# Earlier filter loads, halved last evacuations, a moved inverse piece and a residual added in PSUM, in a two-layer spectral and dense kernel

## The chip, the cores and the metric

One core of one Trainium2 chip. The metric is the device time of one execution in microseconds (us). The kernel before takes 1016.25 us, the median of three runs (1016.15 to 1018.78). "Span" is the same execution as the profiler sees it, some 2 us shorter.

## The reference

Two layers, each a global spectral filter followed by a feed-forward block, all with residuals. 2048 tokens of 1024 features, 3584 hidden features, bf16.

```python
def _A_ref(x, w_r, w_i):                       # the spectral layer
    X = jnp.fft.rfft2(x.astype(jnp.float32), axes=(-2, -1))
    X = X * (w_r + 1j * w_i)
    return jnp.fft.irfft2(X, s=(S, D), axes=(-2, -1)).astype(jnp.bfloat16)

def _B_ref(x, w1, b1, w2):                     # the dense layer
    h = jnp.einsum("bsd,df->bsf", x, w1) + b1
    sp = jnp.log1p(jnp.exp(-jnp.abs(h))) + jnp.where(h > 0, h, jnp.zeros_like(h))
    return jnp.einsum("bsf,fd->bsd", h * jnp.tanh(sp), w2)

x = x + _A_ref(_layernorm(x), A_w_r, A_w_i)
x = x + _B_ref(_layernorm(x), B_w1, B_b1, B_w2)
x = x + _A_ref(_layernorm(x), A_w_r, A_w_i)    # the same weights again
x = x + _B_ref(_layernorm(x), B_w1, B_b1, B_w2)
```

## The kernel before

The spectral layer is a transform in four stages on TensorE, in eight groups. The inverse's first stages (i1, i2) of the last group, number 7, end the steady part. Their output U goes to DRAM and comes back turned (UT), since the last inverse stage (i4) contracts over what U has in its partitions. Group 6 makes the same trip just before:

```python
def u_turn(g, half):
    u = U[g % 3]
    if g == 7:
        h = slice(8 * half, 8 * half + 8)
        if half == 0:
            u_back(6)                          # SyncE: group 6's 512 KB back from DRAM
        self.dma(act, self.u_d[g][:, h, :], u.ap[:, h, :], ...)   # ScalarE: store half of group 7
        if half:
            u_last()                           # six reads of what was stored
    elif half:
        self.dma(sp, self.u_d[g], u.ap, ...)
        if g:
            u_back(g - 1)
```

Each group's PSUM is copied out by one instruction of two banks, on ScalarE or VectorE, and the filter weights of group g + 2 are loaded when group g is done with its buffer (two buffers in turn):

```python
        # i1
            self.op(act, lambda e: e.activation(v.ap[:, :, i, :], src, ACT.Copy), reads=banks, parts=[v.res])
        # i2
            if (g, half) in ((3, 1), (5, 1), (7, 1)):
                self.op(dve, lambda e: e.tensor_copy(dst, ps), reads=banks, parts=[u.res])
            else:
                self.op(act, lambda e: e.activation(dst, ps, ACT.Copy), reads=banks, parts=[u.res])
        # the loop over stages, first layer
                    filter_bins(g)
                    if g < 6:
                        load_w(g + 2)
```

Before i4, TensorE writes the first four token tiles into PSUM as the residual (`residual_first`), and i4 accumulates on them in quarters, as UT's quarters land. The other twelve tiles' columns are done in pieces (`rest`) that fill gaps of the dense layer's start:

```python
        self.spin(8, 0)                        # dummy matmuls, keep TensorE busy
        self.residual_first()
        # ... (cut) ... layer_B starts:
        for u in range(4):
            self.i4(0, 4, 32 * u, 32, 2 * u)
            self.out_first(u, 0, act)
            # ... (cut: statistics)
        for u in range(4):
            self.out_first(u, 2, (act, act, act, dve)[u])
        self.root(0, 2)
        rest(0)
        rest(3)
        for j in range(2):
            xn[j] = self.apply(j)              # normalize
        for j in range(2):
            transposed(0, j, xn[j])            # TensorE transposes, then the first dense matmuls
```

The joint to the second spectral layer: the last token tile's second half is added to the residual by VectorE, its statistics taken, it is normalized, and 16 small copies turn it for the second layer's first stage.

```python
            self.group(fns, reads=ra + r_w2, writes=[self.r_bank[bank]])    # 28 matmuls
            xs = self.XS[:, j, h * 512:(h + 1) * 512]
            self.op(dve, lambda e: e.tensor_tensor(xs, PS[:, bank, :], xs, ALU.add), ...)
            # ... (cut: statistics, then for the last tile)
                b = self.apply(j, out=True)
                self.xr_direct(j, b)           # 16 DMAs on three queues
```

## Time and profile before

In the kernel before (span 1013.1 us):

| stretch, from the trace | us |
|---|---|
| start to the first second-stage matmul ("prologue") | 38.72 |
| from there to the first of the last group's 16 i1 matmuls ("steady", first layer) | 60.72 |
| from there to the first dense matmul ("tail", first layer) | 24.31 |
| first dense layer, to the end of its last product | 395.00 |
| "joint", to the first matmul of the second spectral layer | 7.00 |
| first stage of that layer | 9.91 |
| steady, second layer | 54.70 |
| tail, second layer | 24.49 |
| second dense layer | 395.01 |
| last add and store | 3.21 |

The two dense stretches are 790 us in which TensorE waits for 0.38 us once in each, and otherwise not. The change can only touch the other 223. The view by stretches of 4 us (span of time, its length, busy us and instructions of TensorE, of its weight loads, VectorE, ScalarE and GpSimd, then the granted clock, DMA share, GB/s):

```profile
112.00:116.00 4.00, 2.64 (x86) 2.29 (x85) 0.76 (x2) 0.91 (x2) 0.00 (x0) 0.91 0.32 71
116.00:120.00 4.00, 2.33 (x64) 2.23 (x61) 3.38 (x11) 3.15 (x7) 0.00 (x0) 0.50 0.98 270
120.00:124.00 4.00, 3.06 (x40) 2.87 (x38) 2.58 (x5) 3.54 (x3) 0.00 (x0) 0.73 1.18 293
```

The third number from the right is the clock: half speed from 115.30 to 122.12, while TensorE waits, transposes, and waits again.

### The profile page before, as it was taken

How to read it: one execution, taken by the hardware profiler on the slowest of the kernel's cores; microseconds unless marked ns; L12 is line 12 of the kernel's file. 1: busy time of each engine (PE TensorE's matmuls, PEld its weight loads, DVE VectorE, ACT ScalarE, POOL GpSimd, SP SyncE). 2: the span in 40 equal slices, each digit the busy share in tenths (PEclk: the TensorE clock that was granted, in tenths of full speed). 3: DMA queues.
4: the chain of work that ended last, by engine and by line, in shares of the span. 5: the costliest groups of instructions: out<-in, count | busy, mean ns of one | idle time of the engine just before them, and what ended most of it. 6: DMA issues, size and time to landing. Idle time of an engine off the chain costs nothing.

```text
span 1013.1 us, 13670 instructions
## 1 busy us (share of the span) xinstructions
PE 952.0 (94%) x5749; PEld 506.0 (50%) x5833; DVE 323.9 (32%) x673; ACT 348.7 (34%) x484; POOL 81.6 (8%) x114
## 2 busy tenths in 40 slices
PE   1799799999999999999999978999999999999998
PEld 0576575444444444444456747644444444444443
DVE  7797468002443000033347736830011100000111
ACT  7898474340000343300029848533100023430000
POOL 4651000000000000002421100000000000000000
PEclk9999899999999999999999999999999999999999
DMA  9979813652110220002922875256411212100000
GB/s 284 248 231 321 217 47 115 204 194 61 47 47 30 76 81 21 1 21 90 196 58 83 233 188 156 75 163 201 129 25 45 74 52 83 42 1 11 21 28 25
DMA packets 154205, 107.00 MB, mean 106 GB/s; under 512 B 74448, under 2 KB 133664, under 8 KB 154144
## 3 DMA queue, kind: packets, MB, share of 16 engines
q1 hardware_dynamic: 143056, 78.61, 27.4%
q0 software_dynamic: 8912, 25.84, 8.8%
q10 hardware_dynamic: 2176, 1.66, 0.5%
q8 instruction: 47, 0.77, 0.3%
q14 instruction: 14, 0.11, 0.0%
HBM read 80.85 MB, written 20.71 MB: 100 GB/s over the span
## 4 chain that ended last, share of the span: by engine, by line
PE 87%; DMA 4%; SPq 3%; DVE 2%; ACT 2%; issue 1%; POOL 0%; ACTq 0%; DVEq 0%
PE PS L1067 38%; PE PS L1050 38%; SPq L249 3%; PE PS L771 2%; PE PS L697 2%; PE PS L792 2%; PE PS L961 2%; DMA ARENA<-in_A_w_i_dram 1%; DMA ARENA<-u_scratch 1%; DMA ARENA<-c_bt 1%; DMA u_scratch<-ARENA 1%; PE PS L1016 1%; PE PS L743 1%; ACT ARENA L778 1%; PE PS L810 1%
## 5 line engine op out<-in xcount | busy, mean ns | idle before, releaser
L1050 PE MATMUL PS<-ARENA 128*128 128x512 bf16 (+1 forms) x1950 | 389.1, 358 | 3.8 <-DVE ARENA L1021 1.9
L1067 PE MATMUL PS<-ARENA 128*128 128x512 bf16 x1756 | 385.5, 379 | 1.9
L1054 ACT ACTIVATE ARENA<-PS,B 128x512 bf16<-128x512 f32 (+1 forms) x248 | 159.4, 645 | 412.1 <-PE PS L1050 411.6
L1050 PEld LDWEIGHTS PS<-ARENA 128*128 128x128 bf16 x1984 | 193.0, 98 | 194.7 <-DVE ARENA L1021 2.9
L1067 PEld LDWEIGHTS PS<-ARENA 128*128 128x128 bf16 x1792 | 175.3, 98 | 211.4
L1072 DVE TENSOR_TENSOR XS<-PS,XS 128x512 bf16<-128x512 f32 x64 | 44.3, 692 | 586.9 <-PE PS L1067 586.9
L460 DVE BATCH_NORM_STATS2 BN<-XS 128x6 f32<-128x512 bf16 x100 | 64.6, 674 | 5.4 <-DMA XS<-in_A_x_dram 4.3
L249 POOL DMA_DIRECT2D xn_scratch<-ARENA x12 | 6.5, 541 | 374.2 <-DVE ARENA L512 374.2
L771 PE MATMUL PS<-ARENA 128*128 128x256 bf16 x256 | 32.4, 273 | 4.0 <-DVE ARENA L760 3.2
L778 ACT ACTIVATE ARENA<-PS 128x1024 bf16<-128x1024 f32 x32 | 33.1, 1054 | 6.8 <-PE PS L771 6.8
L432 ACT ACTIVATE RS<-MV,EPS 128x2 f32<-128x2 f32 (+2 forms) x5 | 1.5, 297 | 96.8 <-DVE MV L463 96.2
L697 PE MATMUL PS<-FD,ARENA 128*128 128x256 bf16 (+1 forms) x256 | 31.8, 271 | 2.4 <-ACT ARENA L617 1.2
L749 ACT ACTIVATE ARENA<-PS 128x1024 bf16<-128x1024 f32 x32 | 32.5, 1044 | 4.5 <-PE PS L745 4.5
L771 PEld LDWEIGHTS PS<-ARENA 128*128 128x128 bf16 x256 | 24.2, 98 | 11.8 <-DVE ARENA L760 5.5
L753 DVE TENSOR_TENSOR ARENA<-ARENA 128x1024 bf16<-128x1024 bf16 x32 | 22.0, 688 | 20.4 <-ACT ARENA L749 20.2
L961 PE MATMUL PS<-MT,ARENA 128*128 128x32 bf16 (+1 forms) x512 | 21.4, 199 | 7.1 <-DMA ARENA<-u_scratch 3.8
L697 PEld LDWEIGHTS PS<-FD,ARENA 128*128 128x128 bf16 x256 | 24.4, 98 | 6.5 <-DVE ARENA L619 1.4
L820 ACT ACTIVATE ARENA<-PS 128x1024 bf16<-128x1024 f32 x26 | 26.8, 1066 | 2.4 <-PE PS L792 2.4
L792 PE MATMUL PS<-ARENA,BD 128*128 128x256 bf16 x192 | 24.9, 273 | 2.3 <-ACT ARENA L778 2.3
L512 DVE TENSOR_SCALAR ARENA<-XS,MV,RS 128x1024 bf16<-128x1024 bf16 x48 | 25.0, 545 | 1.0
L961 PEld LDWEIGHTS PS<-MT,ARENA 128*128 128x128 bf16 x512 | 20.0, 102 | 9.8 <-issue 4.5
L732 ACT ACTIVATE ARENA<-PS 128x1024 bf16<-128x1024 f32 x22 | 22.9, 1058 | 3.1 <-PE PS L697 3.1
(79 smaller groups left out, 516.5 us busy)
## 6 DMA issues: line engine op xcount, KB each, us to landing
ARENA<-in_B_w_dram SPq DMA_DIRECT2D x56, 512.0 KB, 3.9
ARENA<-in_B_w_dram SPq DMA_DIRECT2D x56, 256.0 KB, 4.2
u_scratch<-ARENA SPq DMA_DIRECT2D x14, 512.0 KB, 4.4
ARENA<-u_scratch SPq DMA_DIRECT2D x14, 512.0 KB, 6.1
w_scratch<-ARENA POOLq DMA_DIRECT2D x8, 512.0 KB, 5.8
ARENA<-w_scratch POOLq DMA_DIRECT2D x8, 512.0 KB, 5.2
out_dram<-XS SPq DMA_DIRECT2D x16, 256.0 KB, 2.1
ARENA<-xn_scratch POOLq DMA_DIRECT2D x15, 256.0 KB, 10.6
```

What stands on the lines that cost most here:

```text
L249: return eng.dma_start(out_ap, in_ap).then_inc(ds.sem, 16)
L460: self.op(self.dve, lambda e: e.bn_stats(self.BN[:, j, 6 * h:6 * h + 6], self.XS[:, j, 512 * h:512 * h + 512]), reads=[self.r_xs[j]], part ...
L697: fns.append(lambda e: e.matmul(dst, at(r), FD[:, t:t + n], start=start, stop=stop))
L749: self.op(act, lambda e: e.activation(x.ap.rearrange("p a b -> p (a b)"), ps, ACT.Copy, scale=SIG), reads=banks, writes=[x.res])
L771: fns.append(lambda e, c=c, part=part: e.matmul(ps[:, c * 256:(c + 1) * 256], yk.ap[:, part, c * P:(c + 1) * P], t[:, (128, 0)[part]:(384, ...
L778: self.op(act, lambda e: e.activation(v.ap[:, :, i, :], src, ACT.Copy), reads=banks, parts=[v.res])
L792: fns.append(lambda e, dst=dst, part=part, c=c: e.matmul(dst, BD[:, c:c + P], mov(kd, part), start=(part == 0), stop=(part == 1)))
L961: fns.append(lambda e, l=l: e.matmul(self.PS[:, bank + l // k, l % k * w:(l % k + 1) * w], self.UT.ap[:, u0 + l, :], self.MT[:, 8 * lo:8 * ...
L1050: fns.append(lambda e, db=db, bank=bank, fl=fl: e.matmul(PS[:, bank, 0:w], wb.ap[:, db, fl * P:(fl + 1) * P], x.ap[:, db, tok], start=(db ...
L1054: self.op(act, lambda e, bank=bank, ft=ft: e.activation(at.ap[:, ft, tok], PS[:, bank, 0:w], ACT.Mish, bias=self.B1[:, ft:ft + 1]), reads= ...
L1067: fns.append(lambda e, i=i, ft=ft: e.matmul(PS[:, bank, :], at.ap[:, ft, t * P:(t + 1) * P], W2[ft].ap[:, h * 512:(h + 1) * 512], start=(i ...
L1072: self.op(dve, lambda e: e.tensor_tensor(xs, PS[:, bank, :], xs, ALU.add), reads=[self.r_bank[bank]], writes=[self.r_xs[j]])
```

## The change

Four independent pieces, all against waits of a microsecond or less: (a) filter groups 2 and 3 are loaded into free space before the steady part starts, and the spin goes from 8 matmuls to 4; (b) the last group's evacuations of PSUM are split in two halves, one on VectorE and one on ScalarE; (c) one `rest` piece moves behind the first transposes; (d) the last tile's residual is added by one TensorE matmul against the identity, its statistics are read from PSUM, and the normalized tile is written in two halves. The diff, cut to its core (cuts marked):

```diff
 (a)
+    def wr(self, g):
+        return self.WX[g - 2] if g in (2, 3) else self.WR[g % 2]
 ...
+        if li == 0:
+            self.WX = [self.alloc(f"WX{i}", o["UT"] + 4096 * i, [2, 2, 512]) for i in range(2)]
+            for g in (2, 3):
+                load_w(g)
 ...
-                    if g < 6:
+                    if g in (0, 1):
+                        load_w(g + 4)
+                    elif g in (4, 5):
                         load_w(g + 2)
 ...
-        self.spin(8, 0)
+        self.spin(4, 0)
 (b)
+            if g == 7:                         # in i1
+                for b, prog in enumerate((dve, act)):
+                    self.copy(prog, v.ap[:, 4 * b:4 * b + 4, i, :], src[:, 4 * b:4 * b + 4, :], [banks[b]], [], parts=[v.res])
+                return
 ...
+            def last_out(b, prog):             # in i2
+                r = 8 * half + 4 * b
+                self.copy(prog, u.ap[:, r:r + 4, :].rearrange("p a b -> p (a b)"), ps[:, 512 * b:512 * b + 512], [banks[b]], [], parts=[u.res])
 ...
+            if g == 7:
+                last_out(0, dve)
+                last_out(1, act)
+                return
-            if (g, half) in ((3, 1), (5, 1), (7, 1)):
+            if (g, half) in ((3, 1), (5, 1)):
 (c)
         rest(0)
-        rest(3)
         for j in range(2):
             xn[j] = self.apply(j)
         for j in range(2):
             transposed(0, j, xn[j])
         self.warm(ACT.Mish)
+        rest(3)
 (d)
+            summed = not last and (j, h) == (15, 1)
 ...
+            if summed:
+                self.group([lambda e: e.matmul(PS[:, bank, :], self.IDENT[:], self.XS[:, j, 512:1024], start=False, stop=True)],
+                           reads=[self.r_xs[j], self.r_ident], writes=[self.r_bank[bank]])
+                self.finish_last(bank)
+                return
 ...
+    def finish_last(self, bank):
+        self.op(dve, lambda e: e.bn_stats(self.BN[:, j, 6:12], ps), reads=[rb], parts=[r])
+        self.op(dve, lambda e: e.bn_aggr(self.MV[:, j, :], self.BN[:, j, :]), reads=[r], writes=[r])
+        self.root(j, 1)
 ...
+        for h in range(2):
+            src = ps if h else self.XS[:, j, 0:512]
+            self.op(dve, lambda e, h=h, src=src: e.tensor_scalar(..., src, mean, rs, op0=ALU.subtract, op1=ALU.mult), ...)
+            self.xr_direct(j, b, range(4, 16) if h else range(4))
+        self.copy(self.act, self.XS[:, j, 512:1024], ps, [], [rb, self.r_xs[j]])
```

More of the change, by code (lines that the diff above doesn't have):

```diff
@@ L531, in xr_load, with xr_direct @@
                  reads=[self.r_xnd[j]], parts=self.r_xr[1:3])
-    def xr_direct(self, j, b):
-        b.unread = False
-        for i in range(16):
+    def xr_direct(self, j, b, rows):
+        for i in rows:
             half, h = i // 8, i % 8
@@ L541, in xr_direct @@
                      reads=[b.res], parts=[self.r_xr[2 * half]])
+    def finish_last(self, bank):
+        j, dve, ps = 15, self.dve, self.PS[:, bank, :]
+        rb, r = self.r_bank[bank], self.r_mv[15]
+        self.op(dve, lambda e: e.bn_stats(self.BN[:, j, 6:12], ps), reads=[rb], parts=[r])
+        self.op(dve, lambda e: e.bn_aggr(self.MV[:, j, :], self.BN[:, j, :]), reads=[r], writes=[r])
+        self.root(j, 1)
+        b = self.xn_out[0]
+        assert not b.unread
+        mean, rs = self.MV[:, j, 0:1], self.RS[:, 2, j:j + 1]
+        b.res.begin()
+        for h in range(2):
+            src = ps if h else self.XS[:, j, 0:512]
+            self.op(dve, lambda e, h=h, src=src: e.tensor_scalar(b.ap[:, 512 * h:512 * h + 512], src, mean, rs, op0=ALU.subtract, op1=ALU.mult),
+                    reads=[rb if h else self.r_xs[j], r, self.r_rs[j]], parts=[b.res])
+            self.xr_direct(j, b, range(4, 16) if h else range(4))
+        self.copy(self.act, self.XS[:, j, 512:1024], ps, [], [rb, self.r_xs[j]])
     def pair(self):
@@ L661, in load_w @@
         if self.li == 0:
-            self.load_wr(self.WR[g % 2], g)
+            self.load_wr(self.wr(g), g)
             return
@@ L682, in filter_bins @@
             ps, banks, _ = self.pair()
-            self.filter_bins(g, ps, banks, self.WR[g % 2], WT[2 * g % 8:2 * g % 8 + 2], o["WT"] + 2048 * (2 * g % 8),
+            self.filter_bins(g, ps, banks, self.wr(g), WT[2 * g % 8:2 * g % 8 + 2], o["WT"] + 2048 * (2 * g % 8),
                              self.JT, self.r_jt, dve)
@@ L793, in cls @@
                             dst, BD[:, c:c + P], mov(kd, part), start=(part == 0), stop=(part == 1)))
+            def last_out(b, prog):
+                r = 8 * half + 4 * b
+                self.copy(prog, u.ap[:, r:r + 4, :].rearrange("p a b -> p (a b)"), ps[:, 512 * b:512 * b + 512], [banks[b]], [], parts=[u.res])
             if half == 0:
+                u.res.begin()
                 cls(0, ps[:, 0:256], ps[:, 256:512])
+                if g == 7:
+                    self.group(fns, reads=[v.res, self.r_bd], writes=banks[:1])
+                    fns = []
+                    last_out(0, dve)
                 cls(1, ps[:, 512:768], ps[:, 768:1024])
+                if g == 7:
+                    self.group(fns, reads=[v.res, self.r_bd], writes=banks[1:])
+                    last_out(1, act)
+                    return
             else:
@@ L813, in i2 @@
             self.group(fns, reads=[v.res, self.r_bd], writes=banks)
-            if half == 0:
-                u.res.begin()
+            if g == 7:
+                last_out(0, dve)
+                last_out(1, act)
+                return
             dst = u.ap[:, 8 * half:8 * half + 8, :].rearrange("p a b -> p (a b)")
-            if (g, half) in ((3, 1), (5, 1), (7, 1)):
+            if (g, half) in ((3, 1), (5, 1)):
                 self.op(dve, lambda e: e.tensor_copy(dst, ps), reads=banks, parts=[u.res])
@@ L835, in u_turn, with open_ut @@
                     u_back(g - 1)
+        def open_ut():
+            self.UT = self.alloc("UT", o["UT"], [P, P])
+            self.r_ut = self.sub_res(self.UT, "ut", 4, o["UT"], P * P * 2)
+            for r in self.r_ut:
+                r.begin()
         def u_back(g):
+            if self.UT is None:
+                open_ut()
             self.dma(sp, self.UT.ap[g:P:8, :, :], self.u_d[g].rearrange("l r n -> r l n"), f"usp{g % 3}",
@@ L858, in layer_A @@
         U = ring("U", 3, 4 * K, [16, P])
-        self.UT = self.alloc("UT", o["UT"], [P, P])
-        self.r_ut = self.sub_res(self.UT, "ut", 4, o["UT"], P * P * 2)
-        for r in self.r_ut:
-            r.begin()
+        self.UT = None
+        if li == 0:
+            self.WX = [self.alloc(f"WX{i}", o["UT"] + 4096 * i, [2, 2, 512]) for i in range(2)]
+            for g in (2, 3):
+                load_w(g)
         for stage, g, h in self.order_A():
@@ L1068, in mm2 @@
                     PS[:, bank, :], at.ap[:, ft, t * P:(t + 1) * P], W2[ft].ap[:, h * 512:(h + 1) * 512],
-                    start=(i == 0), stop=(i == NF - 1)))
+                    start=(i == 0), stop=(i == NF - 1 and not summed)))
             self.group(fns, reads=ra + r_w2, writes=[self.r_bank[bank]])
+            if summed:
+                self.group([lambda e: e.matmul(PS[:, bank, :], self.IDENT[:], self.XS[:, j, 512:1024], start=False, stop=True)],
+                           reads=[self.r_xs[j], self.r_ident], writes=[self.r_bank[bank]])
+                self.finish_last(bank)
+                return
             xs = self.XS[:, j, h * 512:(h + 1) * 512]
@@ L1084, in mm2 @@
                     self.root(j, 1)
-                b = self.apply(j, out=True)
-                if j == 15:
-                    self.xr_direct(j, b)
-                else:
-                    self.xn_store(j, b)
+                self.xn_store(j, self.apply(j, out=True))
         w2v = self.w2.rearrange("(ft fp) d -> fp ft d", fp=P)
```

## The prediction

> **What bounds the kernel now.** I read the page's engine shares first, then the chain of waits, then the timeline of the stretches where TensorE isn't dense, then the granted clock there by microsecond. The page says that this is a TensorE kernel:
>
> ```profile
> span 1013.1 us, 13670 instructions
> PE 952.0 (94%) x5749; PEld 506.0 (50%) x5833; DVE 323.9 (32%) x673; ACT 348.7 (34%) x484; POOL 81.6 (8%) x114
> PE PS L1067 38%; PE PS L1050 38%; SPq L249 3%; PE PS L771 2%; PE PS L697 2%; PE PS L792 2%; PE PS L961 2%; DMA ARENA<-in_A_w_i_dram 1%; DMA ARENA<-u_scratch 1%; DMA ARENA<-c_bt 1%; DMA u_scratch<-ARENA 1%; PE PS L1016 1%; PE PS L743 1%; ACT ARENA L778 1%; PE PS L810 1%
> ```
>
> The two dense products (L1050, L1067) are 76% of the chain, some 770 us, and the change leaves them alone but for one matmul. All it can win lies in the rest: the two spectral layers (about 0 to 115 us and 519 to 607 us) and their joints. Four places matter. First, the end of the inverse transform, in the chain of waits:
>
> ```profile
> 102.52 1.03 ACT ARENA L778
> 103.59 1.06 PE PS L792 x8
> 104.68 1.03 ACT ARENA L820
> 105.73 2.89 DMA u_scratch<-ARENA
> 110.00 4.54 DMA ARENA<-u_scratch
> 114.67 2.70 PE PS L961 x96
> ```
>
> Nothing overlaps here: each PSUM copy of about 1.03 us is on the path, and the round trip through DRAM follows. The second spectral layer repeats it (593.45 to 606.90). The other half of the last group goes through VectorE, at 105.67:
>
> ```profile
> 105.67 1.23 DVE L818 CAST ARENA<-PS 128x1024 bf16<-128x1024 f32 x1 [4.30 <-PE PS L810]
> ```
>
> Second, the joint from the dense layer to the next spectral layer, again the chain:
>
> ```profile
> 518.86 0.70 DVE XS L1072
> 519.58 0.70 DVE BN L460
> 520.31 0.22 DVE MV L463
> 520.55 0.30 ACT RS L432
> 520.88 0.17 DVE RS L434
> 521.08 0.56 DVE ARENA L512
> 523.16 2.25 DMA ARENA<-ARENA
> 525.75 0.62 PE PS L611 x8
> ```
>
> Third, the wait for filter weights, in the timeline: TensorE waits 1.10, but ScalarE is idle only from 47.84 to 47.94.
>
> ```profile
> 46.71 1.13 ACT L732 ACTIVATE ARENA<-PS 128x1024 bf16<-128x1024 f32 x1
> 47.29 0.62 PE L922 MATMUL PS<-ARENA 128*128 128x256 bf16 x4 [1.10 <-DMA ARENA<-in_A_w_i_dram]
> 47.94 0.87 ACT L937 ACTIVATE ARENA<-PS 128x384 bf16<-128x384 f32 x2
> ```
>
> Fourth, the start of the dense layer, where the clock is the point (columns of the view by stretches: busy of each engine, then the granted clock):
>
> ```profile
> 120.00:121.00 1.00, 1.00 (x16) 1.00 (x14) 0.98 (x2) 0.56 (x1) 0.00 (x0) 0.50 1.12 285
> 611.00:612.00 1.00, 0.71 (x17) 0.72 (x18) 0.97 (x4) 0.92 (x3) 0.00 (x0) 1.00 1.15 340
> ```
>
> The same matmuls (the inverse pieces of 15) ran at half clock in the first layer, at full clock in the second: 30 of them took 2.58 us and 1.45 us.
>
> [...]0.50 from about 115.4 to 122.1 us (two such windows) and from 606.9 to 610.3 (one), each after TensorE had waited for the round trip. [...]the 16 KB copies at the joint take 2.1 to 2.5 us[...]. [...]The trace: 0.63 us for a 128x512 cast from PSUM against 0.55 for twice as many bf16 elements from SBUF.[...]
>
> **The change part by part.**
>
> *Prefetch of filter groups 2 and 3 into free space.* No bytes are saved; two loads issue at about 37.6 us, when the first stage ends, in place of 40.77 and later, so they land near 43.5 and not at 47.16. TensorE's wait of 1.10 us goes. But ScalarE issues its copies back to back from 47.94 to about 68 and would start only 0.10 to 0.2 earlier. I take 0.15 us. The later wait for an inverse table (0.85 us at 78.19) stays: its load, issued at 68.89, is queued behind group 6's load at 67.45, which waits for group 4's buffer before and after.
>
> *Split of the last evacuations, in both spectral layers.* The copy after i1 of the last group: 1.03 becomes about 0.62 (ScalarE's 128x512 takes 0.60, VectorE's 0.63), saving 0.40. For the first of the two i1 copies VectorE is still busy with products until about 101.4, which is before the second one needs it, so no loss. i2's first half: its first bank is ready after four matmuls; ScalarE starts the second bank where it started the pair, and ends in 0.60 and not 1.02: 0.42 more. i2's second half: 0.63 in place of 1.23, minus about 0.15 as ScalarE first issues the first half's store: 0.45. So both stores start about 0.8 earlier, and the three issues and 4.54 us of reading follow rigidly. 0.8 twice is 1.6 us.
>
> *Spin 8 to 4.* It takes 4 x 0.216 = 0.86 us off TensorE ahead of the residual matmuls, which end at 112.24 while the last quarter lands at 114.54. Not on the path: 0.[...]
>
> *Inverse piece moved behind the transposes, both layers.* Second layer, clock up: the old piece ran (0.73 us) while TensorE would have waited for the normalized tile; behind the transposes it fills the wait for VectorE's copy (613.92 to 614.85, 0.93). One gap for another: 0. ScalarE's table load of 1.28 now precedes its copy of 1.36, the same sum before the first Mish. First layer, clock down: TensorE was behind; 15 matmuls at 0.084 = 1.26 us leave the path to the transposes and refill a 0.9 us gap, so about 0.9 to 1.0 is won, limited by ScalarE. The clock state may differ from run to run, so I take half: 0.5.
>
> *Last tile's residual by TensorE.* Adds one 512-wide matmul, 0.22. Removes the add, 0.70 + 0.02. The statistics from PSUM cost the same 0.70 (my estimate from the add's 0.69 and cast's 0.63 with such a source). The scale-and-subtract of 0.56 becomes one of about 0.3 from SBUF, after which four of the sixteen copies are issued, and 0.63 from PSUM. First issue: 521.66 + 0.22 - 0.72 - 0.26 = 520.90. ScalarE's queue issues its first at 520.9, its second at about 521.55 (data ready at about 521.53), its third at about 522.45 against 523.16. That third one carries the chain: 0.7 us won. The copy of the tile to SBUF by ScalarE is queued behind its DMA issues and ends near 525, before ScalarE is wanted at 526.5: 0.
>
> Sum: 0.15 + 1.6 + 0 + 0.5 + 0.7 = 2.95 us. From the median 1016.25: 1013.3 us, a ratio of 0.997.
>
> **The rivals.** (1) *The round trip doesn't follow its start.* The stores at 105.7 share the DMA engines with the previous group's read-back (DMA share 1.2 to 1.3 from 103 to 107). If that sets when the stores land, the 1.6 falls to about 0.6, and the time is near 1014.3. For it: the store took 2.89 in one layer and 3.65 in the other. Against: the stores are large packets on another queue. (2) *The clock gives it back.* Less spinning and an earlier end of the residual matmuls lengthen the idle stretch, [...]and the first dense matmuls (256 wide, 0.109 each) run at half clock: 16 of them cost 1.75 more per layer. Time 1013 to 1017. For it: the clock already fell in both layers, with spinning. Against: it was up again before the dense matmuls both times. (3) *The prefetch is worth its whole wait*, because TensorE and not ScalarE binds from 47 on (it is 95 to 100% busy there), or the loads crowd out the tables. Gain 1.1 or loss 0.5. Time 1012.3 to 1014. The lack of any ScalarE gap speaks against the gain.
>
> **Range and chances.** All terms together, if each goes well (prefetch 1.1, split 2.0, moved piece 1.2, joint 0.9), give 5.2 us, 1011; all going badly with the clock lost gives about 1017. The three runs before spread over 2.6 us. So 1013.3, with 1010.3 to 1015.8 for 8 in 10. Two per cent would be 20 us, and all waits touched are under 15 us together: faster 0.01, within 2% 0.98, slower 0.01.
>
> **What would show it.** Right: the store of the last group starts about 0.8 us sooner after the last products, in both layers; the first matmul of the second spectral layer starts about 0.7 sooner after the last dense matmul; the wait for filter weights is gone while ScalarE's busy stretch begins less than 0.2 sooner; the moved piece lies in the wait before the first dense matmul. Wrong: the read-back lands at the old time (rival 1); the clock column shows 0.50 in the first dense matmuls (rival 2); the stretch from first s2 to last i2 shrinks by over 0.5 in the first spectral layer apart from the split (rival 3); or the statistics from PSUM take much over 0.7.

(The trace of before showed where the granted clock was 0.50, in "windows" of 3.41 us (the falls took 6.83 and 3.41). The split's 1.6 us took for granted that ScalarE and VectorE can each read a bank of PSUM side by side in the time that one alone takes; that was the author's estimate. After shows it nearly so: at 103.67 both start on a 128x512 piece, and take 0.60 and 0.69 us, where single pieces of that size took 0.60 and 0.63 in before.)

## More of the kernel before

A program on one core has no second core to compare with: runs timed in rounds are all of state fast here, single runs of state unknown, and I say which is which.

To find where time moves, I cut each trace at instructions that both kernels have, so that the stretches add up to the span.

## The result, and the profile after

The changed kernel took 1015.36 us (median of 4 runs, 1015.10 to 1016.42) beside 1016.20 for the kernel before (4 runs, 1014.70 to 1018.78). The ratio is 0.9991, with a 95% interval of 0.9969 to 1.0013. Ratios here are the mean time of one kernel's fast runs over that of the other's fast runs of the same rounds, so not quite the ratio of the medians. On another chip, with six and eleven runs, it came to 0.998 (0.9963 to 0.9997), from 1015.97 and 1017.38 us. So the change wins some 1 to 2 us where I said 2.95: within 2%, inside the range, too optimistic. The first interval includes no change at all, the second just excludes it.

The head of the page after:

```profile
span 1013.4 us, 13752 instructions
PE 958.2 (95%) x5826; PEld 506.4 (50%) x5826; DVE 326.5 (32%) x679; ACT 347.7 (34%) x487; POOL 81.5 (8%) x114
```

This profiled run is 0.3 us *longer* than the one of before. One pair of traces can't carry a difference of 0.1%, and the stretches tell why:

| stretch | before | after | difference |
|---|---|---|---|
| prologue (not touched by the change) | 38.72 | 40.07 | +1.35 |
| steady, first layer | 60.72 | 60.52 | -0.20 |
| tail, first layer | 24.31 | 23.54 | -0.77 |
| first dense layer | 395.00 | 395.01 | +0.01 |
| joint | 7.00 | 6.69 | -0.31 |
| first stage and steady, second layer | 64.61 | 64.61 | 0 |
| tail, second layer | 24.49 | 24.73 | +0.24 |
| second dense layer and end | 398.22 | 398.20 | -0.02 |

The prologue hides the gain. It ends with input loads: the first load of token tiles landed at 3.98 us in the one trace and 4.51 in the other, the last of the eight at 13.89 and 15.27. Over fourteen traces of kernels that all share that code, it took from 38.72 to 40.84 us. I leave it out of every comparison below. Without it, the pair shows -1.04 us.

The chain of waits after, at the end of the first inverse transform (start, length, what):

```profile
102.58 1.06 PE PS L793 x8
...
103.67 0.70 DVE ARENA L572
...
104.42 1.06 PE PS L818 x8
...
105.50 0.61 ACT ARENA L568
...
106.18 3.64 DMA u_scratch<-ARENA
...
111.19 4.02 DMA ARENA<-u_scratch
```

Set it beside the same chain in the prediction. The two copies on the path shrank from 1.03 and 1.03 to 0.70 and 0.61, as meant. But the store, 2.89 before, takes 3.64 now. From the first i1 matmul of the last group, the store starts 0.70 us sooner and lands at 9.24 instead of 9.19.

The joint, in the chain of waits:

```profile
514.81 4.33 PE PS L1121 x20
519.14 0.14 issue
519.28 0.39 PE PS L1127
...
521.20 1.15 DVE ARENA L556 x2
522.34 0.02 issue
522.36 0.75 ACTq L249
523.11 0.03 issue
523.14 2.33 DMA ARENA<-ARENA
```

L1127 is the added matmul. The copy that carries the chain starts 4.01 us after the last product's end, 4.41 before. And the wait for filter weights, which was 1.10 at 47.29, is gone from that place; a smaller one appears later, in the timeline (start, busy, line, then in brackets the wait):

```profile
76.04 0.62 PE L975 MATMUL PS<-ARENA 128*128 128x256 bf16 x4 [0.36 <-DMA ARENA<-in_A_w_i_dram]
```

The clock around the start of the first dense layer, by stretches as before:

```profile
112.00:116.00 4.00, 1.60 (x58) 1.56 (x59) 0.75 (x2) 0.60 (x1) 0.00 (x0) 1.00 0.51 114
116.00:120.00 4.00, 2.26 (x79) 2.00 (x75) 2.54 (x8) 2.93 (x6) 0.00 (x0) 0.58 0.62 180
120.00:124.00 4.00, 3.83 (x46) 3.56 (x45) 3.13 (x8) 3.19 (x5) 0.00 (x0) 0.57 1.18 294
```

The moved piece does what it was to do: TensorE is busy 3.83 of the last 4 us, 3.06 before. It still runs at half clock.

### The profile page after: what moved, and what is told of

It reads as the page before. It is cut to its first block, busy times and chain, and to the rows that moved or that the text cites. A ratio compares the mean times of both kernels' runs of the same rounds, so it can differ in the third digit from the quotient of the medians.

```text
span 1013.4 us, 13752 instructions
## 1 busy us (share of the span) xinstructions
PE 958.2 (95%) x5826; PEld 506.4 (50%) x5826; DVE 326.5 (32%) x679; ACT 347.7 (34%) x487; POOL 81.5 (8%) x114
## 4 chain that ended last, share of the span: by engine, by line
PE 87%; DVE 5%; DMA 4%; ACT 2%; POOL 1%; issue 0%; SPq 0%; ACTq 0%; POOLq 0%; DVEq 0%
PE PS L1121 38%; PE PS L1103 38%; PE PS L793 2%; PE PS L719 2%; PE PS L1014 2%; PE PS L818 2%; DMA XS<-in_A_x_dram 1%; DMA ARENA<-c_bt 1%; POOL ARENA L249 1%; PE PS L1069 1%; DMA ARENA<-u_scratch 1%; DVE ARENA L637 1%; DMA u_scratch<-ARENA 1%; DVE ARENA L775 1%; DVE ARENA L610 1%; ACT ARENA L635 1%
## 5 line engine op out<-in xcount | busy, mean ns | idle before, releaser
L771 ACT ACTIVATE ARENA<-PS 128x1024 bf16<-128x1024 f32 x32 | 33.3, 1071 | 4.5 <-PE PS L767 4.5
L804 ACT ACTIVATE ARENA<-PS 128x1024 bf16<-128x1024 f32 x28 | 29.8, 1087 | 3.9 <-PE PS L793 3.9
L568 ACT ACTIVATE ARENA<-PS 128x1440 bf16<-128x1440 f32 (+1 forms) x22 | 25.5, 1160 | 10.8 <-PE PS L793 3.9
L862 ACT ACTIVATE ARENA<-PS 128x1024 bf16<-128x1024 f32 x24 | 25.3, 1090 | 0.0
```

The costliest lines, as they stand in the source:

```text
L771: self.op(act, lambda e: e.activation(x.ap.rearrange("p a b -> p (a b)"), ps, ACT.Copy, scale=SIG), reads=banks, writes=[x.res])
```

## The experiments

Twelve runs followed: nine new kernels and three repeats. All but two compute the right result. One table holds the stretches of all the traces; each experiment then names the column that decides it. "q" is the time from the last group's first i1 matmul to the first of the last 96 of i4's first 128 matmuls, which work on the second, third and fourth quarter of UT; "half" is the time at half clock between 100 and 625 us.

| trace | steady 1 | q 1 | tail 1 | dense 1 | joint | q 2 | tail 2 | dense 2 | half |
|---|---|---|---|---|---|---|---|---|---|
| before | 60.72 | 15.24 | 24.31 | 395.00 | 7.00 | 16.54 | 24.49 | 395.01 | 10.2 |
| after | 60.52 | 14.77 | 23.54 | 395.01 | 6.69 | 16.05 | 24.73 | 395.00 | 17.1 |
| before_again | 61.38 | 15.31 | 24.15 | 395.01 | 7.02 | 16.14 | 25.60 | 397.11 | 17.1 |
| after_again | 60.48 | 14.91 | 23.35 | 395.01 | 6.65 | 15.98 | 24.60 | 395.01 | 17.1 |
| skip_before | 61.75 | 14.77 | 24.29 | 395.01 | 7.02 | 14.39 | 22.84 | 396.81 | 10.2 |
| skip_after | 60.33 | 13.82 | 22.80 | 395.09 | 6.70 | 14.00 | 22.56 | 395.00 | 10.2 |
| split_only | 60.83 | 14.83 | 24.13 | 395.01 | 7.03 | 15.91 | 24.49 | 396.81 | 17.1 |
| merge | 60.44 | 14.75 | 23.42 | 395.46 | 6.13 | 15.89 | 24.24 | 395.78 | 10.2 |
| merge_again | 60.46 | 14.66 | 23.64 | 396.73 | 6.15 | 16.43 | 25.26 | 395.91 | 20.5 |
| pf_spin_back | 60.34 | 14.84 | 23.43 | 395.35 | 6.64 | 16.17 | 24.95 | 395.34 | 10.2 |
| piece_back | 60.41 | 14.64 | 23.79 | 395.01 | 6.67 | 16.24 | 25.41 | 395.01 | 17.1 |
| fill14 | 60.32 | 15.26 | 24.55 | 395.85 | 6.70 | 15.26 | 23.66 | 395.01 | 10.2 |
| combo | 60.32 | 14.66 | 23.12 | 396.19 | 6.15 | 16.32 | 24.16 | 396.18 | 6.8 |
| combo2 | 60.41 | 15.45 | 23.25 | 395.25 | 6.16 | 15.70 | 23.50 | 395.04 | 0 |

(What ends q is the read of the *second* quarter, or the first quarter's matmuls where these are later; the last quarter lands when the others are still being worked on. The texts below speak of the last quarter. In merge, merge_again, combo and combo2 the added matmul of 0.22 us counts in dense 1 and not in the joint. In fill14, combo and combo2, q has more work before it.)

**The theories.** Mine at this point: the split's gain is lost because the store can't land before group 6's read-back, whenever it starts; the joint's because TensorE waits for its own products before the added matmul; and the rest scatters with the clock. The rival for the first: the store is slow by itself. The rival for the last: the clock takes back what the tails win.

### before_again and after_again: the scatter

Both kernels again, unchanged.

> The kernel before once more, for a second trace. Theory (clock windows): the clock windows of 3.41 us run free of the program, so the drop to 0.50 comes at another place than 115.3 and 606.8 us, the two drops of one run are a whole number of windows apart, and the time from the first of the last 96 inverse matmuls to the first dense matmul (9.07 us in the first layer, 7.95 in the second) moves by up to 1.5 us with it. Rival (the times are fixed by the waits): both repeat within 0.2 us. The first s2 matmul (38.72 us) repeats within 0.3 if the prologue is steady, and scatters by about 1 us if the input loads set it.

> The changed kernel once more, with a closer time. From the two traces I count a gain of 1.0 us after the first s2 matmul (0.2 prefetch, 1.8 at the two inverse ends, 0.3 at the joint, 1.3 given back before the second dense layer) and 1.35 us of a later prologue that the change does not touch. If the prologue is scatter, the ratio is about 0.999 and the first s2 matmul is back near 39; if the change caused it, the first s2 matmul stays near 40.1. First i1 of the last group to the first dense matmul: 23.5 and 24.7 us again if the waits fix it, moved by the clock if the windows do.

before_again was a single run (state unknown), 1019.09 us, span 1017.3; the eleven runs of before on that chip spread from 1015.13 to 1021.51. after_again: 1015.97 us (six runs, 1014.58 to 1016.97). What repeats within 0.1 us: the joint (7.02 and 6.65) and everything of the second layer up to its tail. What doesn't: the first steady part of the kernel *before* (60.72, 61.38), and the tails with the clock in them. In before_again the clock fell for 13.65 us in the second layer, and the first dense matmuls ran through it: 397.11 in place of 395.0. Its two falls, at 119.58 and 607.69 us, are 143 times 3.413 us apart, those of before, at 115.30 and 606.82, 144 times: the theory of free-running windows held in these two traces. My test of the prologue came out badly: in after_again it took 39.84 us, near the 40.1 that I would have put down to the change. But piece_back, with the same code there, took 39.12, and skip_before, with nothing of the change, 39.89, so I take it for scatter.

### skip_before and skip_after: what the store waits for

Group 6's read-back is dropped in both kernels. The result is wrong.

```diff
             if g == 7:
                 h = slice(8 * half, 8 * half + 8)
-                if half == 0:
-                    u_back(6)
```

> The kernel before without the read-back of group 6 (wrong result on purpose; its rows of the tile keep old data). In the four traces so far the first store of the last group lands 9.2 us (first layer) and 10.0 us (second) after the first i1 matmul of that group, issued at 6.3 as before or at 5.6 as in the changed kernel, always 0.6 to 0.7 us after the read-back of group 6. Theory (the stores are pinned by that read-back): without it the store lands about 2.2 to 2.5 us after its issue, at about 8.6 to 8.8 in both layers. Rival (a store of this form takes about 2.9 us and more by itself): it lands at 9.2 or later.

> The changed kernel without the read-back of group 6 (wrong result on purpose). Theory (pinned): the store, issued at 5.6, lands at about 7.9 to 8.1, that is 0.7 us sooner than in the kernel before without the read-back, and the last read-back follows by the same 0.7: the split is then worth what was predicted. Rival: no difference between the two, the split is worth nothing in any case.

The first store's piece of the chain, in skip_before and then in skip_after:

```profile
109.14 1.99 DMA u_scratch<-ARENA
111.13 0.02 issue
111.16 4.22 DMA ARENA<-u_scratch
```

```profile
107.72 1.98 DMA u_scratch<-ARENA
109.69 0.02 issue
109.71 4.12 DMA ARENA<-u_scratch
```

(In both, the second half's store ends the chain here; the first half's took 2.03 and 1.99.) Alone, a store takes 2.0 us, and then it does follow its start: it lands at 8.33 in skip_before and 7.59 in skip_after, 0.74 apart, where with the read-back both landed near 9.2. In the second layer the pairs are 8.41 and 8.16, against 10.03 and 10.04. So the store is not slow by itself, and the read-back pins it. The last read lands 0.88 and 0.80 us sooner in skip_after than in skip_before, so without the pin the reads follow the stores as I had predicted.

The trace shows how closely. (Times here count from the last group's first i1 matmul.) The read-back and the store each leave 16 reports of landing in the trace; I read them as one for each of the 16 DMA engines that the page counts, though the records don't name the engine. In the kernel before, second layer, group 6's read-back reports its last three at 8.65, 9.00 and 9.35 us, and the store its last three at 9.21, 9.60 and 10.03; the first thirteen trail in the same way, by 0.43 to 0.49. Where the read's reports are late, the store's are late too. The reports alone don't say whether the store's data starts late or only its report; the trace's packet records (`--dma` with a window, by queue) do. In after, first layer, the store is issued at 5.60 us, and no packet of ScalarE's queue moves before 7.46; in before it is issued at 6.30, and its first packet moves at 7.49. The read-back ends with sixteen packets of 4 bytes, the first of which starts at 7.45 and 7.48, the last at 7.86 and 7.89. Without the read-back the first packet follows the issue by 0.84 us (6.44 in skip_after) and 0.85 (7.15 in skip_before). So the data itself starts late, behind the read-back's. Whether the reports are held up beyond that isn't shown.

The time: single runs of 1017.23 and 1012.83 us (state unknown). skip_after's two tails are together 2.9 us shorter than after's, of the 3.5 us by which its two first stores are shorter (3.64 to 1.99, and 4.44 to 2.56, where one late report comes at 8.16 and the others by 7.59). skip_before's first tail stayed at 24.29, although q came 0.5 sooner; its half clock, from 120.78 to 124.19, fell later than in before.

### split_only: the split by itself

The kernel before with part (b) alone.

> The kernel before with the split of the last evacuations alone. From the first of the last group's inverse matmuls: first store at 5.6 us (before 6.3), landing at 9.2 (first layer) and 10.0 (second), both unchanged since group 6's read-back pins it; the last 96 inverse matmuls start 0.3 to 0.5 us sooner per layer. So the split alone is worth 0.6 to 0.9 us of time, ratio 0.9991 to 0.9994. Rival (the prediction): 1.6 us, ratio 0.9984, with the store landing at 8.4 and 9.2. Joint 7.0, wait for filter weights as before.

1017.09 us (six runs, 1014.59 to 1020.44), ratio 0.9998 (0.9979 to 1.0017). The total can't tell my 0.6 to 0.9 us from the prediction's 1.6; the trace can. The first store starts at 5.60 in both layers (6.30 and 6.38 before) and lands at 9.24 and 10.03 (9.19 and 10.03 before). The gain at the landing is nil. q is 14.83 and 15.91, 0.4 to 0.5 sooner in the first layer; in the second, before itself has 16.54 and 16.14, so there it is 0.2 to 0.6. But it isn't the last quarter that comes sooner: its read lands at 15.51 and 15.47 us in the first layer of before and before_again, and at 15.41 here. What ends q there is the second quarter's read, issued at 10.56 and 10.58, here at 10.61: it lands at 15.10 and 15.18, where its last report comes 0.3 to 0.6 us after the one before it, and here at 14.69. With the split and the unchanged fill, q of the first layer is 14.64 to 14.91 in all seven traces. Why that report is late less often I can't say, nor that the split is the reason: in combo2, which has the split, the read lands at 15.41 again. In the second layer the split's traces (15.89 to 16.43) overlap the two of before, so nothing is shown there. Nor do split_only's own tails, 24.13 and 24.49, differ from before's (24.31 and 24.15; 24.49 and 25.60) by more than the scatter.

### merge and merge_again: the added matmul's wait

The identity matmul goes into the middle of the last product's group and doesn't wait for it:

```diff
-            self.group(fns, reads=ra + r_w2, writes=[self.r_bank[bank]])
             if summed:
-                self.group([lambda e: e.matmul(PS[:, bank, :], self.IDENT[:], self.XS[:, j, 512:1024], start=False, stop=True)], ...)
+                self.group(fns[:14], reads=ra + r_w2, writes=[self.r_bank[bank]])
+                tm = self.group([lambda e: e.matmul(PS[:, bank, :], self.IDENT[:], self.XS[:, j, 512:1024], start=False, stop=False)] + fns[14:],
+                                reads=[self.r_xs[j], self.r_ident] + ra + r_w2)
+                self.r_bank[bank].set_w(self.pe, tm)
                 self.finish_last(bank)
                 return
+            self.group(fns, reads=ra + r_w2, writes=[self.r_bank[bank]])
```

> The changed kernel with the identity matmul put in the middle of the last product's group, so that it no longer waits for the product's own last matmul. Theory: of the joint's 6.68 us (last dense matmul's end to the first matmul of the second spectral layer), about 0.3 is the wait of TensorE for its own result ahead of the added matmul, so the joint falls to about 6.35 to 6.4. Rival: the joint is set by the third issue on ScalarE's queue, which waits for the second scaled half and the issue time before it, and both shift rigidly with the statistics, which gives the same; if they don't (another queue holds), it stays at 6.6 to 6.7. Whole time: 0.3 us less, not to be told from the timing.

> The identity matmul in the middle of the last product's group, as in merge, on another chip. Joint (end of the last main dense matmul to the first matmul of the second spectral layer) 6.13 us again, against 6.65 to 6.69 in the changed kernel, with the added 0.22 us matmul now inside the dense stretch: net 0.3 us. If that is real, the ratio to the kernel before is 0.9963 to 0.9978 and the median about 0.3 us below that of the changed kernel (0.998). Rival: merge's 1014.23 was luck of the clock windows; then the ratio is 0.998 or above, though the joint still reads 6.13.

In the chain of merge the matmul costs its 0.21 and no pause follows, where the changed kernel has an issue pause and 0.39:

```profile
514.86 0.43 PE PS L1121 x2
515.29 0.21 PE PS L1127
515.50 3.04 PE PS L1121 x14
```

The joint is 6.13 and 6.15; with the 0.22 that moved into the dense stretch 6.35 to 6.37, against 6.65 to 6.69: 0.32 us, the same in both. That much of the changed kernel's joint was TensorE waiting for itself. As for the time, merge took 1014.23 us (four runs, ratio 0.9964, 0.9945 to 0.9983) and merge_again 1015.37 (six runs on another chip, ratio 0.9979, 0.9963 to 0.9996). 0.3 us below the changed kernel's 0.998 would be 0.9977: both intervals hold that, and neither shows it; 0.9979 lies between my forecast for merge_again and its rival's. The trace does.

### pf_spin_back: the prefetch

```diff
     def wr(self, g):
-        return self.WX[g - 2] if g in (2, 3) else self.WR[g % 2]
+        return self.WR[g % 2]
 ...  (the early loads of groups 2 and 3 go, the loads in the loop come back)
-        self.spin(4, 0)
+        self.spin(8, 0)
```

> The changed kernel with the prefetch undone and the spin at 8 again. If the prefetch is worth its whole wait: from the first second-stage matmul to the first of the last group's inverse, 60.7 to 61.8 us (before: 60.72, 61.38; skip on the kernel before: 61.75), with the wait for filter weights back at 1 to 2 us. If ScalarE binds there, as the prediction has it: 60.4 to 60.7. In both the stretch from that matmul to the first store stays at 5.6 us, and the last quarter's matmuls start where they do in the changed kernel, within 0.2 us.

The steady part took 60.34 us, as short as any with the prefetch, in a single run of 1014.75 us (state unknown). My expectation that it would return to 60.7 or more failed. So the one run that takes the prefetch out shows no loss. The wait was back, but it was only 0.68:

```profile
47.24 0.61 PE L971 MATMUL PS<-ARENA 128*128 128x256 bf16 x4 [0.68 <-DMA ARENA<-in_A_w_i_dram]
```

Put the five traces without the prefetch in order of that wait: 0.68, 1.10 (before), 1.14 (split_only), 1.78 (before_again), 1.96 (skip_before). Over the mean of the nine with the prefetch, 60.41, their steady parts are longer by -0.07, 0.31, 0.42, 0.97 and 1.34. So some 0.6 to 0.8 us of the wait costs nothing, and what exceeds it costs its full length. The prefetch isn't worth a fixed amount: it takes away a scatter between 0 and 1.3 us, 0.6 on the mean of these five. With it, all nine lie between 60.32 and 60.52. These are single traces, on at least two chips, so the sizes are rough.

### piece_back: the moved piece

```diff
         rest(0)
+        rest(3)
 ...
         self.warm(ACT.Mish)
-        rest(3)
```

> The changed kernel with the inverse piece back ahead of the transposes, all else as changed. Theory (clock): the piece behind the transposes fills TensorE's wait there[...]; with the piece back ahead, [...]the half clock can last 2 to 4 windows into the dense matmuls, as in one trace of the kernel before (13.65 us, 2.1 us lost there). So the runs scatter upward again (some 2 us or more above the lowest), and the mean is 0.5 to 1.5 us above the changed kernel's. Rival (the piece is worth nothing, one gap for another): same mean and spread as the changed kernel, 1014.6 to 1017.

1015.90 us (six runs, 1015.04 to 1017.74), ratio 0.9987 (0.9972 to 1.0001); the changed kernel's 0.998 is inside that interval. The tails are 23.79 and 25.41, against 23.35 to 23.54 and 24.60 to 24.73 in the two traces of the changed kernel. That would be 0.3 and 0.7 us for the moved piece, with both kernels at half clock for 17.1 us. But tails with the piece moved reach 23.64 and 25.26 in merge_again, so the scatter is nearly as large. My theory, half clock that runs on into the dense matmuls, didn't show: both dense stretches are 395.01. What the piece is worth stays open, between 0 and about 1 us in the two layers.

### fill14: dummy matmuls against the clock's fall

Fourteen dummy matmuls before the last residual matmul, so that TensorE doesn't pause before the round trip lands:

```diff
         for b in range(8):
+            if b == 7:
+                self.spin(14, 7)
```

> The changed kernel with 14 more idle-filling matmuls (3.0 us) ahead of the last residual matmul, in the wait for the round trip. Theory (clock): TensorE is busy until about 115 and 605 us, so the drop of the clock comes one window later, after the sparse inverse matmuls have begun; the first dense matmul comes up to 1.5 us sooner where the clock is up during the transposes, but the drop may fall into the dense matmuls instead. Rival (clock does not matter): the first dense matmul comes at the same time after the read-back's arrival as in the changed kernel (8.8 and 9.5 us).

1015.33 us (four runs), ratio 0.9977 (0.9956 to 0.9997): no gain over the changed kernel's 0.998. In the second layer the fall came some 5 us later and the tail shrank by about 1.0 us. Not all of that is the clock: there group 6's read-back landed at 8.71 in place of 9.36, before the fill began, the store at 9.27 in place of 10.04, and q is 0.7 shorter. In the first layer, the fall moved into the dense matmuls, which cost 395.85 in place of 395.01, with a tail of 24.55. The fill in that one place moved the fall to a later one (granted clock 0.88 from 116 to 120 us, 0.50 from 120 to 124, 0.77 from 124 to 128).

### combo and combo2: fill all the gaps

combo joins merge, a fill sized for each layer, and ten inverse columns brought forward into the pause after the first inverse matmuls:

```diff
+            if b == 7:
+                self.spin((8, 16)[self.li], 7)
 ...
+            if u == 0:
+                self.out_first(0, 2, act)
 ...
-        for u in range(4):
+        self.u0 = 10
+        self.i4(4, 12, 0, 10, 0)
+        for u in range(1, 4):
             self.out_first(u, 2, (act, act, act, dve)[u])
 ...
-        rest(0)
+        self.i4_out(4, 12, 0, 10, 0, staged=YS, prog=act)
 ...
-                 rest(6, (10, 10, 3)[fg - 1], dve)
+                 rest(6, (10, 10, 8)[fg - 1], dve)
```

combo2 adds six dummy matmuls in the pause that is left ahead of the transposes (the text says three; the edit has six, and the trace six weight loads for them in each layer):

```diff
+        self.spin(6, 3)
         self.root(0, 2)
```

> A version meant to beat both: the changed kernel with the identity matmul inside the last group, 8 and 16 filling matmuls ahead of the last residual matmul in the first and second layer, and 10 columns of the inverse piece done right after the first inverse, in the wait for the evacuations (two banks are evacuated earlier for it). Theory (clock): [...]the fill and the early piece raise the windows around the read-back from 0.13 to 0.33 to about 0.4, so the half clock is shorter or absent; gain 0.5 to 2 us on top of 0.3 of the joint against the changed kernel, 1012.5 to 1014.5. Rival: the drop only moves into the dense matmuls, as in the first layer of the run with 14 fills, and the time is that of the run with the merged group, 1014.

> The early ten columns and longer fill of combo, with three dummy matmuls more in the gap before the transposes. If thin windows of TensorE cause the clock drops, filling the gaps holds the clock: half clock absent or at most one window of 3.41 us at each spectral layer's end, first dense matmul 23.0 us or less (first layer) and 23.7 or less (second) after the first last-group inverse matmul, dense stretches 395.0 to 395.2 (second about 395.8 with the merged matmul not counted), total 1012 to 1014. Rival: the drop only moves later, into the first dense matmuls, as in combo and fill14: a dense stretch of 395.8 or more in either layer, total 1014.5 or more, ratio about 0.999.

combo: 1016.37 us (six runs), ratio 0.999 (0.9973 to 1.0008). Its trace is at half clock for 6.8 us only, the least of all so far, but at the wrong place, across the first dense matmuls of both layers, 396.19 and 396.18. The rival holds: the fall only moved.

combo2: 1014.22 us (six runs, 1012.37 to 1016.42), ratio 0.9969 (0.9951 to 0.9987), the same chip as combo. Its trace stays at full clock until the last 0.2 us. The stretches of the first tail:

```profile
112.00:116.00 4.00, 3.31 (x42) 1.80 (x40) 0.00 (x0) 0.59 (x1) 0.00 (x0) 1.00 0.54 121
116.00:120.00 4.00, 3.00 (x106) 2.85 (x106) 2.32 (x7) 2.49 (x6) 0.00 (x0) 1.00 0.39 105
120.00:124.00 4.00, 2.75 (x35) 2.00 (x37) 3.64 (x10) 3.52 (x6) 0.00 (x0) 1.00 1.18 305
```

Dense 1 is 395.25, which is 395.01, the added 0.22 and 0.02. The tails are 23.25 and 23.50; I had asked for 23.0 at most in the first and missed by 0.25, and its time is 0.2 above the 1012 to 1014 I gave. The mean granted clock of its six runs is 0.997 to 1.000, of combo's 0.993 to 0.998, of before's twelve on that chip 0.991 to 0.996. Six dummy matmuls a layer (1.3 us at 0.216 each) are all that separates the two kernels; their means differ by 2.2 us (95% interval 0.4 to 4.1). So with *all* the gaps filled the clock could hold, as in this trace, and the rival, that the fall always moves, fell with this run. It doesn't hold it every time: a mean of 0.997 over 1013 us is about 6 us at half clock (0.003 x 1013 / 0.5, my estimate), and two of the six runs have that; two read 1.000. And the gap between the two traces is not all clock: in combo2's second layer group 6's read-back landed at 8.68, in combo's at 9.34, and the six dummies come only after that.

combo2 and merge are the best two. Both intervals overlap that of the changed kernel, so I don't call either shown to be faster than it; against the kernel before both are.

## Why the prediction was right or wrong

The verdict (within 2%) and the range were right; 2.95 us of gain was too much. Neither was a hard test: the range held the kernel before's own fastest run (1014.70), and on the other chip the changed kernel's median, 1015.97, lies just outside it. That 1015.36 fell inside is partly luck. Term by term:

- **Prefetch, 0.15 us: right for the pair, short on the mean.** The pair shows 0.20. The reason given, that ScalarE's work covers most of the wait, fits the free 0.6 to 0.8 us. What failed is taking the one wait of 1.10 in the trace as the wait: it ran from 0.68 to 1.96 over five traces. Rival 3 (the whole wait) is right for the part above 0.7 us.
- **Split, 0.8 us per layer, 1.6 in all: the starts right, "the three issues and 4.54 us of reading follow rigidly" wrong.** The stores start 0.70 and 0.78 sooner, and land at the old time. That is the first rival, and the two skip runs show it. Of 1.6 us the traces show about 0.5 in q of the first layer, where the cause is open, and nothing clear of the scatter in the second; split_only leaves tails and total unchanged within theirs. I had dismissed the rival since "the stores are large packets on another queue". Large they are, 2 KB against 256 bytes for the read-back's, but neither that nor the other queue helped: the store's packets moved only as the read-back's ran out (the first at 7.46 and 7.49 us, the read-back's last at 7.86 and 7.89). I also misread the chain: the 4.54 us of reading that ends at 114.54 is the second quarter's; the last quarter landed at 114.94 and held nothing up.
- **Spin, 0: not separated.** It went back together with the prefetch in pf_spin_back; q was then 14.84 and 16.17, unchanged.
- **Moved piece, 0.5 us: not settled.** It does fill the gap (3.83 of 4 us busy). piece_back gives 0.3 and 0.7 us in one trace, and 0.0007 in the ratio, both within the scatter. That it would be worth nothing in the second layer rested on full clock at that place, as in the one trace I had; in both traces of the changed kernel the clock was at half there (until 614.99 and 614.13).
- **Joint, 0.7 us: the mechanism right, the size half.** It measured 0.31 to 0.37. The first copies were to start 2.15 us after the last main product's end (520.90 less 518.75; before: 2.91) and started at 2.51. The added matmul was put at 0.22 and costs 0.54, as TensorE waits for its own group (0.32, shown by merge). Scaling half a tile took 0.41 from SBUF and 0.81 from PSUM, where I had 0.3 and 0.63. Statistics from PSUM took 0.70, as said.
- **The second rival, the clock.** It is there, in the tails (the second layer's was 0.24 longer in the pair, though q came 0.49 sooner) and sometimes in dense matmuls. The prediction named it, sized only the dense matmuls (1.75 us a layer), and took the falls for the mark of idle windows. That isn't shown: the falls took 6.83 and 3.41 us, two windows and one, but TensorE was busy for 60% and 32% of the windows before them. The kernel before loses as much: in before_again 2.1 us of dense time. I read it as a source of the scatter more than as what takes back this change's gain; the runs don't separate the two.

The measured terms, 0.6 for the prefetch, at most 0.5 for the split, 0.3 for the joint and 0 to 1 for the unsettled piece, make up to some 2.4 us, less what the clock takes. The 1 to 2 us measured fit in that, but the intervals are too wide to prove the sum.

## What to carry to other kernels

Ending an evacuation sooner only pays if what it feeds can go sooner: look whether an earlier, larger DMA is still in flight, on whatever queue, when a store is issued, and when the store's first packet moves (here 1.86 us after the issue with the read-back in flight, 0.84 without). The matmul appended to a group cost a wait of 0.32 us, as it waited for the group; in the middle of the accumulation it cost none. Where an effect is a tenth of a per cent, compare stretches between fixed instructions over several traces, not one pair of spans, and treat TensorE's gaps together: in fill14 and combo, filling some of them moved the clock's fall into the first dense matmuls (395.85 and 396.19 us in the first layer, 395.01 without). Count an experiment's instructions in its trace: combo2 had twice the dummy matmuls that I thought.

## What the traces show, and leave open

- The clock. Here it fell after windows of 3.41 us in which TensorE was partly busy, by sums over the matmul records for 60% and 32% of the time in before, 66% and 13% in after. Three windows of before at 52 to 55% (from 98.23, 105.06 and 596.58 us) kept full clock. At half clock, it came back after windows of 91% and 80% in before and 95% twice in after, and stayed after 60% in before and 49%, 74% and 51% in after. So the busy share of the window before doesn't decide a fall by itself, and no run here finds what does.
- The store. One of 256 KB beside a 512 KB read-back took 3.64 us, alone 1.99, and landed 0.5 to 0.7 us after the read-back whenever it started, with its first packet held from the issue at 5.60 us until 7.46. Why the packets are held isn't shown.
- A matmul that waits for the group before it on TensorE itself: 0.32 us here.
